# A retention layer and a gated MLP on one core: block 2 of the first MLP product goes from plain products to seven, under a new fixed order of all engines

## The chip, the cores and the metric

One core of a Trainium2 chip runs the whole program in one launch. The metric is the device time in microseconds (us), first to last instruction with what the launch adds around it. Five engines work side by side, each through its own list in order: TensorE (PE; its weight loads are PEld), VectorE (DVE), ScalarE (ACT), GpSimd (POOL) and SyncE (SP, which issues most DMAs). Waits between them go by semaphores.

## The reference

```python
scores = scale * np.matmul(q, k.transpose(0, 1, 3, 2))      # 8 batches, 8 heads, 576 x 64
Dmat = np.where(rel >= 0, gamma[:, None, None] ** rel[None, :, :], 0.0)
attn = np.matmul(scores * Dmat, v)                          # causal, decaying weights, no softmax
x = attn.transpose(0, 2, 1, 3).reshape(4608, 512)
h = x @ w_in                                                # 512 -> 2048
g = h * np.cos(h)
out = g @ w_out                                             # 2048 -> 512
```

All inputs and the output are float32.

## The kernel before

**Tiling.** The 4608 tokens are nine blocks of 512. A block is fed by two attention units of 256 tokens (`unit`, `scores`, `outputs`): q, k and v of a unit are loaded by SP (line 585), cast or weighted into `natk`, `qnat`, `natv` (lines 574, 575, 624), transposed (on PE at line 648 for the first four units, by DMA at line 663 for the rest), and multiplied in many small products of 64x64 tiles (line 694): scores (`bk<-qt,kt`), running states (`bk<-natv,natk`), outputs (`bk<-pt,natv`, `bk<-qt,sba` and its like). Two copies per unit write the block's `xt` (lines 574, 575).

**Layer 1** (x @ w_in, then g = h cos h) is made in one of two ways for each block j:

- Plain (`mlp1`, line 908): for each of 16 column groups f, four products over the contraction, 512 tokens wide. Blocks 0 (partly) and 1 are cut into token halves, products of 256. ACT takes the sine with a shift (line 917), DVE multiplies (line 920).
- In seven (`seven1`, line 1037): x and w_in are halved in both directions, and seven products of halves with sums of halves replace eight. A block is four groups g of seven steps of four products of 256, so 112 products. ACT copies three partial sums out of the banks per group (the `seed`, line 968, and two snaps, line 574), DVE adds two back (line 1020), the sines are line 1022, and the product h cos h is on DVE and POOL (line 1026). The sums of x (`xsums`, lines 961 and 963) are four DVE instructions per block.

The sums of w_in (`wsums1`, line 944) are made once: for each of two halves c, T1 and T7 on POOL, T2 and T4 on DVE. T7 is written in place over the slabs 2 and 3 of w_in, which the plain products read, so it waits for the last plain product; T1 carries a read of `xt` of the last plain block. `SEVEN` names the blocks in seven; before it is 3 to 8, and blocks 0, 1, 2 are plain.

**Layer 2** (g @ w_out) is in seven for all blocks (`wino2`, line 1177), with its own sums on DVE (lines 1086, 1108, 1114, 1166).

**Loads of the weights.** Four slabs of w_in and four of w_out (each 128x4x512, cast to bf16 on the way) are DMAs issued by POOL (`load_w`, lines 888 and 892). The loads of the units (0,1) and (1,1), which make block 1, wait for slab 2 of w_in and slabs 1 and 3; those of unit (2,0) wait for slab 2 of w_out.

**What sets the order.** `Graph` collects tasks; `lay` reads a rank for each task from the string `ORDER` (two characters a task), and each engine takes its tasks in rank order. `run` then plays the tasks through with a model of durations (among them `FETCH`, the model of when the next piece of PE's own code is there, `SHARES`, how the two kinds of DMA queues share, and the `dma=` and `tail=` of the slabs). What reaches the chip from that model: which buffer each task gets, how many filler products (`bk<-one`, 128x512, line 517) PE does where the model sees a gap, and which DVE instruction some POOL instructions wait for. The durations themselves reach nothing.

Of the kernel before, what the change touches and what calls it, by code (L numbers as in the profile page):

```python
# [11 lines left out]
B, H, S, D = 8, 8, 576, 64  # L12
# [87 lines left out]
def ap(t, size, p0, n, off, *dims):  # L100
    return bass.AP(t, p0 * size + off, [[size, n]] + [list(d) for d in dims])
# [29 lines left out]
class Graph:  # L131


    BACKLOG, FIRST = 4000, 6000
    SHARES = (0.65, 0.30)
    FETCH = (3200, 1500, 2550, 2000)
    SINCE = 3000

    def __init__(self, pools):
# [83 lines left out]
    def share(cls, hw, sw):  # L223
# [29 lines left out]
    def run(self):  # L253
# [3 lines left out]
        seen, usable, whole = 4, {}, [False] * 8  # L257
        dma_free, port_free = 2500.0, {"dve": 0.0, "pool": 0.0}
# [41 lines left out]
        while len(order) < len(self.tasks):  # L300
            s, e = min(((x, i) for i, x in ((e, due(e)) for e in free if todo[e]) if x is not None), key=lambda c: c[0], default=(0, None))
            if e is None:
                raise RuntimeError(f"the order is stuck: {[(e, todo[e][-1].name, [b.pool for b in todo[e][-1].allocs]) for e in free if todo[e]]}")
            t = todo[e].pop()
# [33 lines left out]
            if t.dma is not None:  # L338
                both = both and not (len(sw) == slow and ends[1][-1] < s)
                if not both:  # L340
                    dma_free = max(dma_free, s + 1750) + t.dma
                    done = dma_free + t.tail
                else:
# [11 lines left out]
                    if hw:  # L355
                        dma_free = ends[0][-1]
# [15 lines left out]
class Kernel:  # L372
# [43 lines left out]
    GATE = 'k'
    TXENG = ("pool", "dve", "pool", "dve")
# [480 lines left out]
    def mlp1(self, j, f, ses, prio):  # L898

# [25 lines left out]
    def wsums1(self):  # L925
# [12 lines left out]
        for c in range(2):  # L938
            for eng, i, x, y, r in (
# [4 lines left out]
                self.one(eng, 2150 if eng == "pool" else 660, lambda e, i=i, c=c, x=x, y=y: e.tensor_tensor(t(i, c), x(), y(), ALU.subtract),  # L944
                         r=r + self.xkeys(self.SEVEN[0] - 1, (0, 1)), w=keys(i, c), port=True, name=f"T{i}")

# [287 lines left out]
    def graph(self):  # L1234
# [116 lines left out]
```

## Time and profile before

| what | us |
|---|---|
| median of 3 runs | 282.84 (282.12 to 283.46) |
| the profiled execution, whole | 284.13 |
| its span, first to last instruction | 282.4 |
| PE matmul busy / PE weight load busy | 270.7 / 219.9 |
| DVE / ACT / POOL busy | 227.3 / 177.5 / 161.2 |
| HBM read and written | 36.70 MB, 9.44 MB |

The granted TensorE clock is 1.000 throughout. A row of the profile names the line, the engine, the tile written and the tiles read, the shape and the count; a time in brackets is idle time ahead of the group and what ended it. The chain of work that ended last goes back from the last instruction, at each step to what released it; its pieces in order of time show a start, a length and a name. "issue" means the engine waited for nothing that the profile shows. Matmul records overlap, so a rate is best read from the chain: the length of a run of products over their number.

### The profile page before, as it was taken

The numbers are of one execution on the slowest core, as the hardware profiler recorded it, in microseconds if no ns is written. First come the engines' busy times: TensorE is split into PE (matmuls) and PEld (weight loads), VectorE is DVE, ScalarE is ACT, GpSimd is POOL, SyncE is SP. The second block draws the span as 40 slices with busy tenths as digits, with TensorE's granted clock in tenths as the row PEclk, the third lists the DMA queues.
The fourth block names the chain that finished last, engine by engine and source line by source line (L and its number), as shares of the span: only waits on it lengthen the run. The fifth ranks groups of instructions, "written<-read, shape, count | busy, mean of one in ns | idle before, by whom it ended". The sixth has DMA issues, their size and how long they took to land.

```text
span 282.4 us, 9745 instructions
## 1 busy us (share of the span) xinstructions
PE 270.7 (96%) x4136; PEld 219.9 (78%) x4136; DVE 227.3 (80%) x394; ACT 177.5 (63%) x367; POOL 161.2 (57%) x180
## 2 busy tenths in 40 slices
PE   6779989999999999979999999999999999999995
PEld 2457568888885468868888888888888888888884
DVE  3666889988974998868997996688759899997764
ACT  4346767255247765669469875885778865778530
POOL 4640872167377683897568757981375667216330
DMA  7999999999999999999999997979816090410016
GB/s 199 249 192 262 273 171 163 300 243 263 179 187 245 204 264 206 181 221 176 251 192 208 279 238 134 168 194 175 194 32 123 6 163 2 159 69 0 2 74 224
DMA packets 122731, 49.91 MB, mean 177 GB/s; under 512 B 84800, under 2 KB 118592, under 8 KB 122688
## 3 DMA queue, kind: packets, MB, share of 16 engines
q1 hardware_dynamic: 118176, 44.84, 74.8%
q0 software_dynamic: 4224, 4.19, 9.6%
q8 instruction: 32, 0.52, 0.8%
q10 hardware_dynamic: 288, 0.26, 0.3%
q14 instruction: 11, 0.09, 0.1%
HBM read 36.70 MB, written 9.44 MB: 163 GB/s over the span
## 4 chain that ended last, share of the span: by engine, by line
PE 84%; DMA 8%; POOL 3%; issue 2%; SPq 1%; DVE 1%; ACT 1%; DVEq 0%; ACTq 0%
PE bk L1177 38%; PE bk L1037 26%; PE bk L908 11%; PE bk L694 8%; DMA stgq<-in_q_dram 3%; DMA win<-in_moe_w_in_dram 3%; DMA stgk<-in_k_dram 3%; POOL natv L624 1%; SPq L585 1%; POOL qnat L624 1%; POOL gt L1026 1%; POOL win L888 0%; ACT xt L574 0%; DVE sq L1020 0%; PE bk L648 0%
## 5 line engine op out<-in xcount | busy, mean ns | idle before, releaser
L1026 POOL TENSOR_TENSOR gt<-sq,cb 128x512 bf16<-128x512 f32 x48 | 55.8, 1172 | 49.1 <-ACT cb L1022 27.0
L908 PE MATMUL bk<-xt,win 128*128 128x256 bf16 (+1 forms) x288 | 46.3, 308 | 1.8 <-DMA win<-in_moe_w_in_dram 0.9
L624 POOL TENSOR_TENSOR natv<-stgv,wv 128x512 bf16<-128x512 f32 x36 | 37.5, 1046 | 12.5 <-DVE s L1108 4.8
L920 DVE TENSOR_TENSOR gt<-bk,cb 128x256 bf16<-128x256 f32 (+1 forms) x72 | 34.5, 507 | 12.0 <-ACT cb L917 9.3
L917 ACT ACTIVATE cb<-bk 128x256 bf16<-128x256 f32 (+1 forms) x72 | 31.2, 455 | 19.6 <-PE bk L908 16.5
L624 POOL TENSOR_TENSOR qnat<-stgq,wq 128x512 bf16<-128x512 f32 x32 | 33.5, 1052 | 16.7 <-DVE s L1114 5.6
L1037 PE MATMUL bk<-xt,win 128*128 128x256 bf16 x288 | 41.0, 273 | 0.0
L1020 DVE TENSOR_TENSOR sq<-bk,sq 128x512 f32<-128x512 f32 x48 | 32.5, 684 | 8.9 <-PE bk L1037 5.0
L908 PEld LDWEIGHTS bk<-xt,win 128*128 128x128 bf16 x288 | 26.8, 98 | 15.3 <-DVE pt L743 1.2
L743 DVE TENSOR_TENSOR pt<-bk,tr 128x512 bf16<-128x512 f32 x48 | 31.1, 682 | 8.4 <-PE bk L694 8.1
L575 POOL CAST natk<-stgk 128x512 bf16<-128x512 f32 x34 | 20.7, 614 | 28.2 <-DMA stgk<-in_k_dram 15.7
L1177 PE MATMUL bk<-wout,gt 128*128 128x256 bf16 x288 | 36.7, 273 | 0.0
L1026 DVE TENSOR_TENSOR gt<-bk,cb 128x512 bf16<-128x512 f32 x48 | 32.3, 682 | 4.0 <-ACT cb L1022 3.8
L1177 PE MATMUL bk<-wout,s 128*128 128x256 bf16 x288 | 35.6, 273 | 0.0
L1177 PE MATMUL bk<-tw,s 128*128 128x256 bf16 x288 | 35.4, 273 | 0.0
L574 ACT ACTIVATE sq<-bk 128x512 f32<-128x512 f32 x48 | 27.7, 595 | 10.0 <-PE bk L1037 8.8
L1022 ACT ACTIVATE cb<-sq 128x512 bf16<-128x512 f32 x48 | 30.0, 632 | 5.4 <-DVE sq L1020 2.9
L1022 ACT ACTIVATE cb<-bk 128x512 bf16<-128x512 f32 x48 | 28.4, 598 | 6.7 <-PE bk L1037 3.7
L1177 PEld LDWEIGHTS bk<-tw,s 128*128 128x128 bf16 x288 | 28.0, 98 | 3.6 <-DVE pt L743 0.3
L1037 PEld LDWEIGHTS bk<-xt,win 128*128 128x128 bf16 x288 | 27.9, 98 | 3.6
L1177 PEld LDWEIGHTS bk<-wout,gt 128*128 128x128 bf16 x288 | 27.6, 98 | 3.7 <-issue 0.2
L1177 PEld LDWEIGHTS bk<-wout,s 128*128 128x128 bf16 x288 | 27.7, 98 | 3.5
(80 smaller groups left out, 436.5 us busy)
## 6 DMA issues: line engine op xcount, KB each, us to landing
stgq<-in_q_dram SPq DMA_DIRECT2D x16, 512.0 KB, 6.1
out_dram<-os SPq DMA_DIRECT2D x16, 512.0 KB, 4.4
stgk<-in_k_dram SPq DMA_DIRECT2D x20, 256.0 KB, 5.6
stgv<-in_v_dram SPq DMA_DIRECT2D x20, 256.0 KB, 5.4
stgk<-in_k_dram SPq DMA_DIRECT2D x6, 512.0 KB, 6.9
stgv<-in_v_dram SPq DMA_DIRECT2D x6, 512.0 KB, 7.4
win<-in_moe_w_in_dram POOLq DMA_DIRECT2D x4, 512.0 KB, 8.0
wout<-in_moe_w_out_dram POOLq DMA_DIRECT2D x4, 512.0 KB, 7.5
```

The costliest lines, as they stand in the source:

```text
L574: return self.one(eng, dur, lambda e: e.activation(dst(), src(), AF.Copy), r=r, w=w, **kw)
L624: self.one(eng, 610 if eng == "dve" else 1030, lambda e, out=out, inp=inp, tab=tab, col=col, hs=hs: e.tensor_tensor(out(), inp(), ap(tab, ...
L694: return lambda e: e.matmul(out(), lhs(), rhs(), start=start, stop=True, skip_group_check=True)
L743: self.one("dve", 610, lambda e, r=r, b=b, pt=pt: e.tensor_tensor(ap(self.at(pt), 1024, 0, 128, 512 * r, [64 * ny * ny, 8 // ny // ny], [1 ...
L908: inst = e.matmul(ap(self.at(bk), 512, 0, 128, 0, [1, n]), ap(self.WIN, 4 * DFF, 0, 128, c * DFF + 128 * f, [1, 128]), ap(self.at(xt), 204 ...
L917: self.one("act", n - 15, lambda e: e.activation(ap(self.at(cb), TB, 0, 128, 0, [1, n]), ap(self.at(bk), 512, 0, 128, 0, [1, n]), AF.Sin, ...
L920: self.one("dve", 75 + n / 0.96, lambda e: e.tensor_tensor(ap(self.at(gt), NF * TB, 0, 128, f * TB + 256 * h0, [1, n]), ap(self.at(bk), 51 ...
L1020: self.one("dve", 610, lambda e: e.tensor_tensor(half(src), self.at(bank).ap(), half(src), ALU.add), r=[(bank,)], w=four(src))
L1022: self.one("act", 530 if name else 490, lambda e: e.activation(self.at(cb).ap(), ap(self.at(src), size, 0, 128, 0, [1, 512]), AF.Sin, bias ...
L1026: self.one(eng, 1120 if name else 610, lambda e: e.tensor_tensor(ap(self.at(gt), NF * TB, 0, 128, (8 * n + 2 * g) * TB + 256 * h, [TB, 2], ...
L1037: inst = e.matmul(ap(self.at(bank), 512, 0, 128, 256 * f, [1, 256]), l(c, f), rr(c), stop=True, skip_group_check=True, start=(first and f ...
L1177: inst = e.matmul(place(bank, tt), l(f, tt), rr(f), stop=True, skip_group_check=True, start=(first and f == 0 and tt < len(bank)))
```

## The change

`SEVEN` gains block 2. So its 64 plain products of 512 go, and 112 products of 256 come, with the copies, adds and sums of `seven1` and `xsums`; `wsums1` now has to be done a block earlier, after block 1 in place of block 2. `ORDER` is a new table for every engine and every task. `FETCH`, `SHARES` and the slab durations are new numbers of the model. Lines of the changed file are one higher than those of before (`seven1` is 1038 in place of 1037).

```diff
-    BACKLOG, FIRST = 4000, 6000
-    SHARES = (0.65, 0.30)
-    FETCH = (3200, 1500, 2550, 2000)
+    BACKLOG = 4000
+    SHARES = (0.80, 0.35)
+    FETCH = (3200, 1500, 3550, 5550)
...
-                    usable[k] = max(a + self.FETCH[0], dma_free + self.FETCH[1]) + self.FETCH[2] + self.FETCH[3] * (a < 45000)
+                    usable[k] = max(a + self.FETCH[0], dma_free + self.FETCH[1]) + self.FETCH[2 + (a < 45000)]
...
-    SEVEN = (3, 4, 5, 6, 7, 8)
+    SEVEN = (2, 3, 4, 5, 6, 7, 8)
...
-        "#####$#$#$#%#%#$#######%#&#&#%#$#&#'#)#(#'#)#,#+#'#.#7#/#*#/#'#+#*#,#(#-#.#&#&#%#*#)#(#-#(#)#*#0#2#0#1#3"
+        "#####$###$#$#&#$#####&#%#%#%#&#$#'#'#(#-#)#*#+#-#)#/#0#0#*#/#%#'#(#)#'#*#,#'#&#&#+#(#,#.#(#,#*#.#1#0#2#1"
...
-                 sem=f"{which}{s}", dma=2750 if which == "win" else 3000, tail=900, prio=prio)
+                 sem=f"{which}{s}", dma=3350 if which == "win" else 3450, tail=500, prio=prio)
```

The order on PE where block 1 begins. In before, after the outputs of unit (0,1), PE does a few plain products of block 0, one transpose of `qnat`, and then the plain products of block 1's first token half:

```order
L908 MATMUL bk<-xt,win 128x256 x4
L648 MATMUL bk<-idn,qnat 128x128 x4
L908 MATMUL bk<-xt,win 128x256 x28
L648 MATMUL bk<-idn,natk 128x128 x4
L908 MATMUL bk<-xt,win 128x256 x4
L1177 MATMUL bk<-wout,gt 128x256 x8
```

In the changed kernel block 0 is finished ahead of those outputs, and three transposes of unit (1,1) stand between them and block 1:

```order
L649 MATMUL bk<-idn,qnat 128x128 x4
L649 MATMUL bk<-idn,natk 128x128 x8
L909 MATMUL bk<-xt,win 128x256 x12
L695 MATMUL bk<-natv,natk 64x64 x16
L909 MATMUL bk<-xt,win 128x256 x20
L649 MATMUL bk<-idn,qnat 128x128 x4
```

So the transposes of `natk` moved ahead of block 1, into the place right after the outputs.

POOL around the sums of w_in (`tx<-win` is T1, `win<-win` is T7). In before they are spread among the casts of the units of blocks 3 to 5, and the last of the four stands a little further on:

```order
L624 TENSOR_TENSOR qnat<-stgq,wq 128x512
L944 TENSOR_TENSOR tx<-win 128x1024
L624 TENSOR_TENSOR qnat<-stgq,wq 128x512
L575 CAST natk<-stgk 128x512
L624 TENSOR_TENSOR qnat<-stgq,wq 128x512
L624 TENSOR_TENSOR natv<-stgv,wv 128x512
L575 CAST natk<-stgk 128x512
L624 TENSOR_TENSOR qnat<-stgq,wq 128x512
L624 TENSOR_TENSOR natv<-stgv,wv 128x512
L944 TENSOR_TENSOR win<-win 128x1024
```

In the changed kernel all four stand close together:

```order
L945 TENSOR_TENSOR tx<-win 128x1024
L576 CAST natk<-stgk 128x512 x2
L625 TENSOR_TENSOR qnat<-stgq,wq 128x512 x2
L576 CAST natk<-stgk 128x512
L945 TENSOR_TENSOR win<-win 128x1024
L625 TENSOR_TENSOR qnat<-stgq,wq 128x512 x2
L945 TENSOR_TENSOR tx<-win 128x1024
L625 TENSOR_TENSOR natv<-stgv,wv 128x512
L945 TENSOR_TENSOR win<-win 128x1024
```

So they moved some twelve POOL instructions forward, and eight POOL instructions of the seven products (line 1027) come behind them.

PE in the stage of block 2, where attention crowds most. In before (the scores and states of a unit between runs of products):

```order
L1177 MATMUL bk<-wout,s 128x256 x16
L1037 MATMUL bk<-xt,win 128x256 x4
L1037 MATMUL bk<-xs,tx 128x256 x4
L694 MATMUL bk<-qt,kt 64x64 x32
L694 MATMUL bk<-natv,natk 64x64 x16
L1037 MATMUL bk<-xt,tx 128x256 x4
L1037 MATMUL bk<-xs,tx 128x256 x4
```

In the changed kernel, behind the 80 small products of one unit's outputs and ahead of the 80 of the next, whose first 32 are the last row:

```order
L1038 MATMUL bk<-xt,win 128x256 x4
L1038 MATMUL bk<-xs,tx 128x256 x4
L1178 MATMUL bk<-wout,gt 128x256 x16
L695 MATMUL bk<-qt,kt 64x64 x32
L695 MATMUL bk<-natv,natk 64x64 x16
L1038 MATMUL bk<-xt,tx 128x256 x4
L1038 MATMUL bk<-xs,win 128x256 x4
L695 MATMUL bk<-pt,natv 64x64 x32
```

So between two runs of 80 small products there are now 48 small and 32 large ones, and between a unit's scores and its own outputs eight large ones.

More of the change, by code (lines that the diff above doesn't have):

```diff
@@ new lines @@
+        "#3#5#-#7#9#8#1#7#%#(#+#)#.#-#H#A#I#H#*#/#0#K#C#M#I#+#2#1#)#O#Q#K#L#N#O#P#G#T#S#U#J#S#,#7#6#X#N#W#K#-#;#4"
+        "#b#U#V#P#.#8#9#2#.#8#G#B#G#4#+#4#D#?#D#6#/#6#E#>#E#3#,#5#;#4#=#:#3#:#A#;#?#S#I#Q#>#7#@#9#2#9#=#6#;#<#5#<"
+        "#B#<#A#F#@#F#J#D#J#R#H#R#N#F#M#@#:#B#L#E#P#C#=#C#?#8#>#3#5#:#<#/#=#>#2#D#C#0#@#?#7#j#s#m#o#r#s#\\#\\#w#n#x"
+        "#a#b#]#b#i#k#`#j#w#n#Y#L#T$,#p$($.#r$+$-#q$*#u#`#v#|#e#|#p#^#p$+#s$,#e#X#c$/#t$-#q#_#u$$#g#z#Z#M#Y$0#u$."
+        "#[#O#W$1#v$0#f#Y#e$##i$##]#Q#X$4#w$1#a#T#^$2#x$2#`#W#_$'#k$$#y#c#y$%#h#{#_#V#d$*#o$'#z#d#x$)#m$)#^#R#Z$("
@@ new lines @@
+        "#l$%#V#[#U#\\#g#a#f#h#c#d#Z#k#m#l#i#n#]#g#h#[#r#t#t#l#o#q#Q#{$&#j#>#3#F#H#5#K#J#1#A#B#;$3$6$8$/$3$:#v#f$>"
+        "#{$#$?#|$$#6#8#I#L#:#O#N#9#4#Q#E#@#?#<#S#W#C#U#V#=#G#T#Z#H$=$A$>$=$?$@$F$)$,$G$($*$N$K$M$/$0$W$7$9$d$E$H"
+        "$e$F$Y#B#A#]#`#E#d#^#D#F#[#h#P#K#I#a#i#M#j#l#J#S#b#m#W$j$]$^$J$K$m$U$V$n$N$a#G$&#M$O#P$B#R$P$F$G$I$J$C$&"
+        "$K$+$E$'$E$M$.$R$N$6#Y$O$L$4#X$[$;$T$P$1$Q$2$X$8$S$S$3$V$Q$B#_$T$R$=#\\$]$>$W$U$5$\\$<$Y$@$X$Z$:$^$U$I#c$_"
+        "$V$P#f$a$C$_$`$?$g$G$c$D$Z$b$A$f$\\$M#e$l$`$R#g$k$L$b$4$6$5$7$;$C$<$A$7$8#y$5$9$9$;$<#z$:$@$%$B$D$D$H$J$H"
@@ new lines @@
+        "#N$I$L$-#v$c$e$g$h$o$O$r$S$q$T$m$s$W$w$o$_#n$u$j$[#r%$$Z$u%&$]%'$b%*$g$y%)$a%-$x$m#w%.$w$f#s%2$i$z%/$e%1"
+        "$h%3$k${%4$l%8%$$u#z%5%#$q#y%>$x%.%7$n%9$o%:$p%)%=$t%A%+${$#%<%'$y#|%E$z%2$[$f$d$i$k$t$l$s$h$i$Q$t$z$n$v"
+        "$x$X$p$y$Y${$|$p%0%6$|#\\%%%($`#Z%#$r$q$\\$^%+$j$d%,$c$v#O#L#k#q#R#u#t#U#_#o$$#]#V#T#p#x#Y#{$&#X#`#v$%#i%;"
+        "%%%&$s$r%?%%%,%@$v%(%*%,%0%/%C$w%I%#%H%$%6%G$|%K%3%1$,%L%5%+$*%N%'%=%Q%)%R%*%U%.%>%T%-%Z%C%5$.%Y%B%;$1%b"
+        "%8%F%\\%4%`%7%c%:%H%a%9%h%J%F$7%d%G%B$6%l%D%O%f%=%m%E%i%?%K%j%@%n%N%M$8%s%U%S$:%r%H%T%-%1%4%8%:%9%;%<%B%D"
@@ new lines @@
+        "%&%F%J%7%O%S%/%M%P%(%[%_%E%V%W%?#y%e%g%>#o%X%@%A%0%2%]%<%3%^%6%D#[#b$($2#^$+$'#e#d$0$)#l#a#c$/$-#h$9$5#f"
+        "#g$3$4#t%k%M%L%A%C%p%I%L%q%G%P%Q%S%W%V%t%J%v%P%w%N%X%x%O%{%]%V$?%|%\\%h$H&(%[%g&'%U&/%Z&+%Y%d&*%X&-%f%\\$A"
+        "&2%h%b$E&3%^%j&4%_&6%c&7%g%q&8%d&;%p%q$J&<%o%p$K&@%m%z&>%i&B%l&A%k%s&E%o&I%y%v$L&F%x%z$M&M%w&#%I%R%[%_%e"
+        "%`%b%a%o%u%K&)&,%c%y&.%]&#&&%W&5&9%l&0&1%i$.&=&?%j$4%z%Z%Y%Q%R&$%`%a&%%T%^#j#s$>$=#k$@$<#n#u$;$B#{#m#q$C"
+        "$G#r$I$D#p$*$F$N$(&:%m%n%e%f&C%s%{&D%n%t%u%w%{%v&G%r&L%u&K%y&&&N%x&Q&'&&$P&R&(%|$X&W&)&/&Y&'&Z&(&^&,&1&\\"
@@ new lines @@
+        "&*&`&2&.$S&]&0&/$U&f&3&6&d&0&h&4&j&6&<&g&5&l&:&;$[&k&9&=$]&r&@&D&m&8&p&<&x&F&H&q&:&w&B&C$^&u&A&I$_&|&D&F"
+        "%k%|&$&%%r&.&,&-&H&J%t&S&U&)&P&T&%&O&X&+&[&_&4&c&e&5$6&s&t&?$:&V&*&+&#&$&a&-&1&b&2&3$+#z#w#x$R$W#|$)$2$0"
+        "$V$Y$,$/$$$'$Q$O$;&i&7&8&7&n&o&9&;&=&>&C&?&v&>&y&A&z&B&E&{&E''&L&M$a'#&J&O$c'0&P&P'$&H'%&G')&J&K'*&K'.&M"
+        "&N$e'+&S&W$f'2&S&R',&L'6&V'/&U&U'1&Q'5&V&b$i';&Y&]$g'<&d&g'>&Y'?&Z'A&[&^'B&\\'E&f&f$j'C&`&^$h'O&h&m&@&I&G"
+        "&N&Q&Z&O&]'('3&T'4'7&T'8'9&X'&'-&R'='@&\\'H'J&h$?'D'F&_$A$%$-$#$&$T$Z$9$5$3$8$\\$`$1$=$7$<$d$b$>':&_&X&[&W"
@@ L415 @@
+        "'G&`&b&a&c&d&e&j&l'I&c'N&g'M&j&p'L&e'S&o&q$l'Q&n&l$k'V&p&x'R&i'T&k'Y&n&t'X&m']&v&t$m'W&s&x$n'b&v&{'Z&r'\\"
+        "&s'a'$'+'_&u'e'#'#$o'`&z'-$r'k'('-'c&w'i&z'h&|'''g&{'m'(''$p'l')'*$q'p'&',&a&k&r&w&i&q'$&y'P'U&o'K'[&u'^"
+        "'f&y'd'o'%'j'n'*'r't'/$@'s'w',$C&|'&'0'1'%'2'.'5'q'v')'+'u'|'3$F$B'y'z'/'.'x'{'0(#($'4'6$D$E(%(''8'1'2(&"
+        "(('7'9$G$H"
     )
```

28 lines of the change are left out of this document (removed).

## The prediction

> **What bounds the kernel now.** I read the page's busy times and slices first.
>
> ```profile
> span 282.4 us, 9745 instructions
> PE 270.7 (96%) x4136; PEld 219.9 (78%) x4136; DVE 227.3 (80%) x394; ACT 177.5 (63%) x367; POOL 161.2 (57%) x180
> PE   6779989999999999979999999999999999999995
> ```
>
> PE is below 9 tenths only in the first slices, once in the middle, and at the very end. The windows say how much is idle where (PE, PEld, DVE, ACT, POOL busy, then clock, DMA share, GB/s).
>
> ```profile
> 30.00:40.00 10.00, 8.85 (x161) 5.47 (x160) 8.31 (x17) 5.80 (x12) 9.77 (x12) 1.00 1.01 218
> ...
> 60.00:70.00 10.00, 10.00 (x93) 8.78 (x92) 9.27 (x21) 5.25 (x16) 5.75 (x7) 1.00 1.08 256
> 70.00:80.00 10.00, 9.97 (x218) 8.16 (x217) 9.79 (x17) 4.30 (x10) 4.32 (x6) 1.00 1.11 180
> ...
> 120.00:130.00 10.00, 8.54 (x247) 7.23 (x240) 7.01 (x12) 7.78 (x17) 8.54 (x10) 1.00 1.16 188
> ```
>
> The last idle of the start ends by 40 us, and after that the one hole over half a us is that of 120 to 130. Busy time alone would not prove it, since ends of matmuls are modelled; so I take the chain of waits in order of time.
>
> ```profile
> 12.95 8.27 DMA win<-in_moe_w_in_dram
> ...
> 21.70 8.43 DMA stgq<-in_q_dram
> 30.13 0.08 issue
> 30.21 1.76 POOL qnat L624 x2
> 31.97 0.26 issue
> 32.23 2.05 POOL natv L624 x2
> ...
> 37.51 0.71 issue
> ...
> 38.69 0.76 ACT xt L574
> 39.45 0.12 issue
> 39.57 3.22 PE bk L908 x28
> ...
> 69.50 0.44 PE bk L908 x4
> ...
> 85.55 3.45 PE bk L908 x16
> ...
> 123.99 1.46 issue
> ...
> 175.67 3.06 PE bk L1037 x28
> ```
>
> Up to 39.57 the chain runs through DMAs (a slab of w_in, then q of unit (0,1)) and POOL; from there it is PE almost without a break. The end is therefore the time at which block 1's first product starts, plus PE's work behind it, plus its few stalls.
>
> **The change, part by part.** All sums are against the profiled execution, 284.13 us whole, 1.29 above the median of 282.84; I carry the difference over to the median.
>
> *PE's work.* A 512-wide product costs 3.45/16 = 0.2156 us, a 256-wide one 3.06/28 = 0.1093 us. Removed: 64 x 0.2156 = 13.80. Added: 112 x 0.1093 = 12.24. So **-1.56 us**, all of it behind 39.57. The seeds of bank contents that the seven products need are ACT copies, not PE work. (The Trainium skill, "TensorE: Matmul & The Clock Gate", section "Back-to-back issue gap", speaks against the change: it gives a sustained stream about 131 ns for a product of 512 and 81 ns for one of 128, so width comes cheap. With some 98 ns between them for 256, an estimate from that page, the sum would be 112 x 98 - 64 x 131 = +2.6 us. This trace disagrees with it: 216 ns and 109 ns.)
>
> *The start.* The same eight slab and unit loads precede the first product of block 1. On POOL the second slab is now issued behind one cast (0.61) and one `natv` half (1.05, both by the page's groups below), the first slab ahead of a cast. PE gets there with more done: block 0 is finished and the transposes of `natk` are behind it, in what was idle of 30 to 40, where the window shows 1.15 us; two more 512-wide fillers and two more changes between small and large products lie in that idle too. I take **0** for the time of 39.57, with -0.6 (one cast earlier) to +1.66 (cast and `natv` in full) as bounds.
>
> *Work beside PE.* Durations by form:
>
> ```profile
> L1022 ACT ACTIVATE cb<-sq 128x512 bf16<-128x512 f32 x48 | 30.0, 632 | 5.4 <-DVE sq L1020 2.9 <-POOL gt L1026 1.8 <-DVE gt L1026 0.5
> ...
> L574 ACT ACTIVATE sq<-bk 128x512 f32<-128x512 f32 x48 | 27.7, 595 | 10.0 <-PE bk L1037 8.8 <-POOL gt L1026 1.2
> L1026 POOL TENSOR_TENSOR gt<-sq,cb 128x512 bf16<-128x512 f32 x48 | 55.8, 1172 | 49.1 <-ACT cb L1022 27.0 <-DVE xs L961 8.2 <-DVE s L1114 7.8
> L624 POOL TENSOR_TENSOR natv<-stgv,wv 128x512 bf16<-128x512 f32 x36 | 37.5, 1046 | 12.5 <-DVE s L1108 4.8 <-DVE s L1114 3.8 <-DMA stgv<-in_v_dram 2.5
> L575 POOL CAST natk<-stgk 128x512 bf16<-128x512 f32 x34 | 20.7, 614 | 28.2 <-DMA stgk<-in_k_dram 15.7 <-DVE pt L743 7.0 <-DVE s L1114 2.4
> ...
> L944 POOL TENSOR_TENSOR tx<-win 128x1024 bf16<-128x1024 bf16 x2 | 4.3, 2127 | 0.0
> ```
>
> ACT: the number of sines stays at 16, and 12 copies come: 12 x 0.595 = +7.1 us. POOL: 8 x 1.172 = +9.4 us. DVE: 16 products before, 8 products and 8 adds after, the same, and the four sums of x, about +2. ACT and POOL are at 63% and 57%, DVE at 80%; PE waits for none of them as long as each result is there in time, so **0**.
>
> *The sums of w_in, a block earlier.* T7 can't start before the last plain product of block 1, which in before ends at 69.50 + 0.44 = 69.94. By the order rows POOL then has T7, two `qnat`, T1, one `natv`, T7: 3 x 2.13 + 3 x 1.05 = 9.5 us, to about 79.5. By PE's order 112 products of 256 and 200 small ones of attention stand between the last plain product and the first that reads these sums.
>
> ```profile
> 77.28 1.30 PE bk L694 x76
> ```
>
> That is 112 x 0.1093 + 200 x 1.30/76 = 12.2 + 3.4 = 15.6 us, so the sums are needed near 85.6. Margin 6 us; POOL's queue behind T7 (casts for units of later blocks) has the idle of 60 to 80, where it is 5.75 and 4.32 busy of 10. So **0**; if the cover went, each us beyond the six would cost one.
>
> *Code.* PE's own instructions come in by DMA while it runs.
>
> ```profile
> q8 instruction: 32, 0.52, 0.8%
> ```
>
> That is 32 packets for 2 x 4136 instructions, 258 each, or 129 products. A piece that is late shows as "issue". The hole of 120 to 130 is such a one. One such packet passes in the 1.3 us of 122.6 to 123.9 (first row below, the queue's share of that stretch), and PE goes on behind it:
>
> ```profile
> q8 instruction: 1, 0.02, 5.5%
> ```
>
> ```profile
> 125.45 0.25 PE L694 MATMUL bk<-natv,natk 64*64 64x64 bf16 x7 [1.46 <-issue]
> ```
>
> The two of the start, 0.71 at 37.51 and another near 20, look alike. Density decides together with luck: 247 products in 120 to 130 stalled, 218 in 70 to 80 did not. In the changed order, the outputs of two units and the scores of one crowd: 80 + 8 + 16 + 48 + 8 + 80 products, 240, in
>
> ```profile
> 104.31 0.91 PE bk L694 x80
> ...
> 113.63 0.51 PE bk L694 x48
> ```
>
> 2 x 0.91 + 0.51 + 32 x 0.109 = 5.8 us. That is nearly two pieces of code in 5.8 us, where before had its densest ones at about 20 products per us (x218 in 10, x247 with a stall). So I expect a stall there, near 100 us, in place of the one at 124. Bounds: 0 (no piece late) to 2 x 1.46 = 2.9 (two late in a row). I take 1.5 times the one row, 2.2, since two pieces are in question and one stall gives the next piece time: **+0.7** against the 1.46 of before.
>
> *A unit's outputs close behind its scores.* The eight large products between them take 0.87; DVE needs two masks, which in before began 0.22 after PE.
>
> ```profile
> 114.20 1.29 DVE L743 TENSOR_TENSOR pt<-bk,tr 128x512 bf16<-128x512 f32 x2 [0.22 <-PE bk L694]
> ```
>
> 0.22 + 1.29 = 1.51, less 0.87 and about 0.2 for the states between: 0.4 us of wait, but inside the stretch where the code is late, so I count none of it beside that; bounds 0 and 0.4.
>
> The sum: -1.56 + 0 + 0.7 = **-0.9 us**, 283.2 profiled, **281.9** median.
>
> **The rivals.**
>
> *The code comes in time.* Then the 1.46 of before goes as well: -1.56 - 1.46 = -3.0, 279.8 (and any time between that and the forecast, if one piece is a little late). For it: of the stretches above, only one of before stalled past 40 us, and a planner that reckons with later code should leave more room. Against it: the 240 products in 5.8 us. (The Trainium skill, "Runtime: NRT & Kernel Launch", section "Instruction fetch mechanics", says the refill of 16 KiB blocks of 256 instructions is mostly hidden, and by it there would be no stall. The trace agrees on the size, 0.52 MB in 32 packets, and disagrees on the rest, by 1.46 us.) It shows as no "issue" over 0.5 us after 40. Everything faster than 281.4 belongs here: **0.34**.
>
> *Code late more often.* The other side: the same mechanism at four pieces, the two in the crowded stretch and two in later ones (before has the like of the x205 here). 4 x 1.46 = 5.8; against 1.46 that is +4.4, with -1.56 it is +2.8: 285.6. It decides from two more late pieces on, since 2 x 1.46 is above 1.56. For it: the DMA share is above 1 in that row (1.27) as in most up to 170, so a packet has a queue ahead of it.
>
> ```profile
> 150.00:160.00 10.00, 9.80 (x205) 8.32 (x203) 8.75 (x13) 9.34 (x21) 7.99 (x9) 1.00 1.27 212
> ```
>
> Against it: one late piece shifts PE and gives the next more time. **0.17**.
>
> *POOL late with T7*, over its 6 us: the seven products of block 2 stand and everything with them; 10 us late gives +4 - 1.56 = +2.4, 285.2. The margin speaks against it: **0.02**.
>
> *Wide products cheaper than two narrow ones.* In a stream a product can't be below its weight load, 219.9/4136 = 0.053 on average; if the 64 wide ones in truth cost half of 0.2156 each, the change would lose 12.24 - 6.9 = +5.3. The 16 in 3.45 us exclude it nearly: **0.02**.
>
> *The start is late* by 1.66 us, which eats the gain of PE: 282.84 + 0.8 = 283.6, within 0.5% of before, **0.03**.
>
> **How the numbers follow.** Forecast 0.42, code in time 0.34, code late more often 0.17, POOL 0.02, wide products 0.02, late start 0.03. A measurement of this kernel can tell about 0.5%, 1.41 us, from no change. Faster than 281.4: 0.34. Slower than 284.25: 0.17 + 0.02 + 0.02 = 0.21. Within: 0.45. The forecast's own range goes from -1.56 - 0.6 (start) - 0.5 (a stall of about 1 in place of 1.46) = -2.7 to -1.56 + 1.44 (two late pieces) + 0.4 (masks) + 0.4 (a quarter of the start's bound) = +0.7, so 280.2 to 283.5; to hold 8 in 10 it takes in most of the faster rival, down to 280.0, and half of the slower, up to 284.8.
>
> **What would show it.** Right: in the chain, products of line 1038 at 0.109 us in the stage of block 2; the first product of block 1 within 0.6 of 39.57; PE without idle behind it but for "issue" near 100; the hole of DVE in 80 to 90, in which the plain block of before left it 4.61 busy of 10, filled.
>
> ```profile
> 80.00:90.00 10.00, 10.00 (x171) 6.92 (x170) 4.61 (x8) 4.89 (x11) 8.22 (x8) 1.00 1.18 222
> ```
>
> Wrong: PE waiting for POOL `win` or DVE `tx` near 86 (the sums late), for DVE `pt` by over 0.4, or a slab of w_in that lands after 22.5.

## The result, and the profile after

The changed kernel took 286.67 us in the median of 4 runs (284.91 to 286.94), the kernel before 283.15 in 4 runs beside it (282.12 to 283.50): a ratio of 1.0107, 95% interval 1.0068 to 1.0146. It is slower, by about 3.0 us. The prediction said 281.9, with a range of 280.0 to 284.8. The profiled execution took 286.94, its span is 285.2.

The head of the page of the changed kernel:

```profile
span 285.2 us, 9866 instructions
PE 273.6 (96%) x4186; PEld 224.0 (79%) x4186; DVE 231.3 (81%) x398; ACT 183.2 (64%) x379; POOL 171.7 (60%) x188
PE   7879999999999999999999999999999999999995
PE 75%; DVE 10%; DMA 5%; ACT 3%; POOL 2%; issue 2%; SPq 1%; DVEq 0%; POOLq 0%
```

PE is still busy 96% of the time, and the slices look full. What has changed is the last line, the shares of the chain that ended last. In before it read

```profile
PE 84%; DMA 8%; POOL 3%; issue 2%; SPq 1%; DVE 1%; ACT 1%; DVEq 0%; ACTq 0%
```

So 10% of the chain now goes through DVE and 3% through ACT, where it was 1% each. A share of the chain is not lost time: part of it lies near 130 to 144 and 187 to 199 us, where PE loses only 0.45 and 0.26. Windows of the changed kernel, most of them those of the prediction (PE, PEld, DVE, ACT, POOL busy, clock, DMA share, GB/s):

```profile
60.00:70.00 10.00, 9.74 (x103) 8.24 (x100) 6.80 (x18) 8.06 (x22) 8.74 (x9) 1.00 1.02 202
70.00:80.00 10.00, 9.71 (x188) 7.76 (x176) 9.95 (x16) 2.65 (x7) 5.34 (x6) 1.00 1.09 231
80.00:90.00 10.00, 9.84 (x199) 8.15 (x197) 9.19 (x15) 6.52 (x15) 6.76 (x5) 1.00 0.99 184
90.00:100.00 10.00, 9.52 (x141) 7.41 (x141) 8.95 (x14) 9.01 (x20) 9.12 (x10) 1.00 1.01 213
100.00:110.00 10.00, 9.02 (x244) 6.96 (x232) 9.02 (x15) 8.61 (x18) 7.45 (x8) 1.00 0.91 196
120.00:130.00 10.00, 9.98 (x185) 8.06 (x185) 6.43 (x11) 8.82 (x19) 9.26 (x10) 1.00 1.15 176
```

The hole of 120 to 130 is gone. In its place there are short ones from 60 to 110 us, and from 90 to 110, where block 2 is now made in seven, DVE and ACT are near nine tenths, and POOL is up to 100 us. What PE waits for behind 45 us, from the waits of the changed kernel (idle us in all, times, longest):

```profile
PE bk L695 <- issue: 0.7, 1, 0.7
PE bk L1178 <- DVE s L1109: 0.5, 2, 0.3
PE bk L695 <- DVE pt L744: 0.4, 1, 0.4
PE bk L1038 <- issue: 0.3, 1, 0.3
PE bk L909 <- DVE gt L921: 0.3, 1, 0.3
PE bk L1038 <- ACT sq L575: 0.2, 1, 0.2
PE bk L1038 <- ACT bk L969: 0.2, 1, 0.2
PE bk L1038 <- DVE sq L1021: 0.2, 1, 0.2
PE bk L695 <- ACT xt L575: 0.2, 1, 0.2
```

In before there was one row:

```profile
PE bk L694 <- issue: 1.7, 2, 1.5
```

These lists are short of the truth, since the modelled ends of matmuls cover part of each wait (the 0.69 of code near 162 is 0.87 by the starts). So I add up from the starts of all products: what lies between one start and the next, less the length of a product (0.1092 for 256, 0.0108 and 0.0165 for the small ones, and so on) and less 0.1 at each change between small and large ones, is **lost time**. The sums below are worked out from these starts; a small negative one only means that the mean length is a little high. Two profiles of each kernel (the second ones are experiments 9 and 5 below):

| us | before | before, again | changed | changed, again |
|---|---|---|---|---|
| first product of block 1 | 39.57 | 39.30 | 40.34 | 39.31 |
| lengths of all products from there | 232.26 | 232.26 | 230.18 | 230.18 |
| changes between small and large (60 and 64) | 6.0 | 6.0 | 6.4 | 6.4 |
| lost up to 45 | 0.12 | 0.12 | 0.22 | 0.22 |
| lost 45 to 80 | 0.32 | 0.35 | 1.04 | 1.82 |
| lost 80 to 110 | -0.15 | -0.33 | 2.35 | 2.00 |
| lost 110 to 170 | 1.31 | 0.67 | 1.24 | 1.45 |
| lost behind 170 | -0.03 | -0.07 | 0.01 | -0.10 |
| start of the last product | 279.28 | 278.20 | 281.68 | 281.18 |
| span | 282.4 | 281.3 | 285.2 | 284.7 |

Means of the two: start +0.4, lengths -2.1, changes +0.4, lost time +4.0 (1.16 to 5.13), last product to end +0.4; together +3.1, as the spans have it (281.85 to 284.95). The gain on PE came as forecast, and was eaten nearly twice over by lost time, most of it between 45 and 110 us. Not all of that is waiting for DVE and ACT: of the 2.35 from 80 to 110 us, 0.48 is a piece of PE's code that came late at 109.13 ("issue"), and 0.49 is the masks (DVE `pt` at 105.28). About 1.4 is left for copies, seeds, adds and sums.

The chain of the changed kernel names the places:

```profile
72.71 2.44 DVE s L1109 x3
...
93.52 2.74 PE bk L1038 x24
...
96.27 0.61 ACT sq L575
...
98.01 0.59 ACT bk L969
...
103.94 1.29 DVE pt L744 x2
...
161.68 0.69 issue
...
216.87 4.80 PE bk L1038 x44
```

From 40 us on before's chain was PE and a little issue, but for 259 to 264 us, where it ran through DVE, POOL and ACT. Here it leaves PE for a sum of layer 2 on DVE (72.71), a copy out of a bank (96.27), a seed (98.01), the masks (103.94). The last row is the rate of seven products where nothing disturbs them: 4.80/44 = 0.109 us.

### The profile page after: what moved, and what is told of

It is laid out like the page before. It is cut to its first block, busy times and chain, and to the rows that moved or that the text cites. A ratio compares the mean times of both kernels' runs of the same rounds, so it can differ in the third digit from the quotient of the medians.

```text
span 285.2 us, 9866 instructions
## 1 busy us (share of the span) xinstructions
PE 273.6 (96%) x4186; PEld 224.0 (79%) x4186; DVE 231.3 (81%) x398; ACT 183.2 (64%) x379; POOL 171.7 (60%) x188
## 4 chain that ended last, share of the span: by engine, by line
PE 75%; DVE 10%; DMA 5%; ACT 3%; POOL 2%; issue 2%; SPq 1%; DVEq 0%; POOLq 0%
PE bk L1178 33%; PE bk L1038 26%; PE bk L909 9%; PE bk L695 7%; DMA win<-in_moe_w_in_dram 3%; DMA stgv<-in_v_dram 2%; DVE s L1109 2%; DVE pt L744 2%; POOL gt L1027 1%; DVE xs L962 1%; DVE sq L1021 1%; ACT cb L1023 1%; ACT sq L575 1%; SPq L586 1%; ACT xt L575 1%
## 5 line engine op out<-in xcount | busy, mean ns | idle before, releaser
L1027 POOL TENSOR_TENSOR gt<-sq,cb 128x512 bf16<-128x512 f32 x56 | 65.2, 1169 | 47.4 <-ACT cb L1023 23.6
L1038 PE MATMUL bk<-xt,win 128*128 128x256 bf16 x336 | 48.9, 273 | 0.2 <-DVE sq L1021 0.2
L1027 DVE TENSOR_TENSOR gt<-bk,cb 128x512 bf16<-128x512 f32 x56 | 38.1, 683 | 8.1 <-ACT cb L1023 6.0
L575 ACT ACTIVATE sq<-bk 128x512 f32<-128x512 f32 x56 | 33.1, 602 | 9.3 <-PE bk L1038 8.1
L1023 ACT ACTIVATE cb<-sq 128x512 bf16<-128x512 f32 x56 | 35.2, 634 | 5.6 <-DVE sq L1021 4.4
L1038 PEld LDWEIGHTS bk<-xt,win 128*128 128x128 bf16 x336 | 31.6, 98 | 5.3 <-DVE sq L1021 0.3
L1038 PE MATMUL bk<-xs,tx 128*128 128x256 bf16 x224 | 33.2, 273 | 0.6 <-issue 0.3
L909 PE MATMUL bk<-xt,win 128*128 128x256 bf16 (+1 forms) x224 | 31.1, 288 | 2.4 <-DVE gt L921 1.1
L575 ACT ACTIVATE sn<-bk 128x512 f32<-128x512 f32 (+1 forms) x29 | 16.4, 568 | 25.0 <-PE bk L1178 21.2
L918 ACT ACTIVATE cb<-bk 128x256 bf16<-128x256 f32 (+1 forms) x56 | 22.3, 416 | 14.5 <-PE bk L909 11.3
```

The lines of the kernel that those rows point to most:

```text
L575: return self.one(eng, dur, lambda e: e.activation(dst(), src(), AF.Copy), r=r, w=w, **kw)
L909: inst = e.matmul(ap(self.at(bk), 512, 0, 128, 0, [1, n]), ap(self.WIN, 4 * DFF, 0, 128, c * DFF + 128 * f, [1, 128]), ap(self.at(xt), 204 ...
L918: self.one("act", n - 15, lambda e: e.activation(ap(self.at(cb), TB, 0, 128, 0, [1, n]), ap(self.at(bk), 512, 0, 128, 0, [1, n]), AF.Sin, ...
L1023: self.one("act", 530 if name else 490, lambda e: e.activation(self.at(cb).ap(), ap(self.at(src), size, 0, 128, 0, [1, 512]), AF.Sin, bias ...
L1027: self.one(eng, 1120 if name else 610, lambda e: e.tensor_tensor(ap(self.at(gt), NF * TB, 0, 128, (8 * n + 2 * g) * TB + 256 * h, [TB, 2], ...
L1038: inst = e.matmul(ap(self.at(bank), 512, 0, 128, 256 * f, [1, 256]), l(c, f), rr(c), stop=True, skip_group_check=True, start=(first and f ...
```

## The experiments

**Theory A**: the changed kernel loses its gain, and more, in short waits of PE for DVE and ACT, because the seven products' copies, adds and products come into a stage where both engines have no room; one further cause is a POOL instruction that holds up a bf16 sum on DVE. **Rival B**: late code. **Rival C**: 112 products of 256 cost PE more than their count says. A further rival came up on the way: the new order, and not block 2 in seven, makes the waits. Ratios are to the kernel before, run beside it on the same chip, with the 95% interval; "lost" is the sum above, of the one execution that was profiled. Where a kernel leaves out work, the expectation says so.

**1. T7 ahead of the cast.** POOL's order:

```diff
 L625 TENSOR_TENSOR qnat<-stgq,wq 128x512 x2
-L576 CAST natk<-stgk 128x512
 L945 TENSOR_TENSOR win<-win 128x1024
+L576 CAST natk<-stgk 128x512
```

> The changed kernel with one place changed in POOL's order: the first T7 stands ahead of the cast of natk that waits for its DMA, not behind it. Theory A (PE of the changed kernel loses its gain in short waits for DVE and ACT, at 66 to 82 us and at 93 to 107 us; one cause is a POOL instruction that holds up a bf16 sum on DVE): the first sum of layer 2 of block 1 falls from 1.85 us to about 0.7, and the excess of 0.32 and 0.33 us ahead of PE's products at 75.7 and 78.1 goes: 0.6 us less in the profile at 80 us, ratio to before about 1.008 in place of 1.0107. Rival B (late code makes the loss): the two waits stay or come back as others, no gain. Rival C (the 112 products themselves are slower than the 64): no gain.

Between 71 and 76 us the first two sums of layer 2 of block 1 and T7 stand like this in the changed kernel (busy, mean ns of one):

```profile
L1109 DVE TENSOR_TENSOR s<-gt 128x1024 bf16<-128x1024 bf16 x2 | 2.4, 1262 | 0.0
L945 POOL TENSOR_TENSOR win<-win 128x1024 bf16<-128x1024 bf16 x1 | 2.1, 2121 | 0.0
...
L576 POOL CAST natk<-stgk 128x512 bf16<-128x512 f32 x1 | 0.6, 611 | 1.0 <-DMA stgk<-in_k_dram 1.0
```

and in this kernel

```profile
L1109 DVE TENSOR_TENSOR s<-gt 128x1024 bf16<-128x1024 bf16 x2 | 1.3, 684 | 0.0
```

Lost from 45 to 80: 0.17 in place of 1.04; from 80 to 110 it is 2.32, as before the edit. Ratio 1.0091 (1.0058 to 1.0124), within the interval of the changed kernel. So T7, put off by 1.0 us by a load of k, did stretch the sum by 2 x (1.262 - 0.684) = 1.2 us, and the two waits behind it went. But experiments 2 and 4 have the old place and lose 0.30 and 0.17 there: with a load that lands earlier the collision doesn't happen; the cast does not stand there, and the pair of sums takes 1.28 us in both. It is a cost of some executions, not the cause of the 3 us.

**2. Adds of block 2 cut.**

```diff
-self.one("dve", 610, lambda e: e.tensor_tensor(half(src), self.at(bank).ap(), half(src), ALU.add),
+m = 32 if j == 2 else 512
+self.one("dve", 610, lambda e: e.tensor_tensor(  # columns 0 to m of the same three
```

> The changed kernel with the eight adds of block 2's seven products on DVE cut to 32 of 512 columns (most of those two sums per group is left out): about 8 x 0.6 = 4.8 us less work on DVE between 88 and 108 us. Theory A, DVE being what is late there: the excess at 105.3 (0.59, the masks) and 106.5 (0.40, an add) goes, and part of that at 98.6: 0.8 to 1.2 us less. Theory A, ACT being what is late: less than 0.3. Rival B: the waits for code at 109.1 and 162.4 (0.48 and 0.87) stay and nothing else matters: within 0.3. Rival C: no gain.

Ratio 1.0084 (1.0055 to 1.0114); lost from 80 to 110: 2.02 against 2.35. The masks' wait stays (0.49), the seed's too. Some 4.8 us less for DVE (14.55 busy of 20 from 90 to 110 in place of 17.97) is not enough; the expectation that DVE alone is late is wrong.

**3. Sines and snaps of block 2 cut.**

```diff
+m = 64 if j == 2 and g > 1 else 512     # snaps: columns copied
+w = 64 if j == 2 and g > 0 else 512     # sines: columns
```

> The changed kernel with block 2's sines of groups 1 to 3 and snaps of groups 2 and 3 cut to 64 of 512 columns (most of g h cos h of these is left out): 12 x 0.5 + 4 x 0.5 = 8 us less work on ACT between 91 and 108 us. Theory A with ACT late: the excess at 96.9 (0.41, a snap) and 98.6 (0.40, a seed) goes, 0.8 us less. Theory A with DVE late: these shrink little, under 0.3. Rival B and rival C: no gain.

Ratio 1.0066 (1.0037 to 1.0094), lost from 80 to 110: 2.14. The wait for a snap at 96.9 went, the others stayed, and the late code at 109 is 0.69 here. ACT's sines alone aren't it either: ACT is 12.35 busy of 20 from 90 to 110, as little as in before (12.51), and most of the loss is still there.

**4. Code shifted by 32 products.**

```diff
+extra = 0 if self.shifted else 32
+self.shifted = True
 def mm(e):
+    for _ in range(extra):
+        e.matmul(...)   # bk<-one, 128x64
     for _ in range(n):
```

> The changed kernel with 32 tiny products more at the very start, where PE idles, so that every later piece of PE's code begins 32 products earlier in the program. Rival B: the late piece at 162.4 gets 7.0 us of PE work between its request and its use in place of 5.5, so its 0.87 us go, and the one at 109.1 (5.4 us, as before) stays: 0.8 us less, ratio about 1.008. Theory A: as rival B for these 0.87 us, and all other waits stay; over 2 us of the loss remain. If the time falls by more than 1.5 us, theory A is wrong.

Ratio 1.0137 (1.0101 to 1.0174): not faster. The two waits for code, 0.32 at 109.13 and 0.69 at 162.37 in the changed kernel, are two larger ones here:

```profile
106.04 0.22 PE L701 MATMUL bk<-qt,sbb 64*64 64x64 bf16 x2 [1.32 <-issue]
```

```profile
173.77 0.49 PE L1184 MATMUL bk<-wout,gt 128*128 128x256 bf16 x3 [0.90 <-issue]
```

The late piece at 162 did go, as rival B has it, but others came, so the shift moved the late code and did not remove it. The masks' wait (0.49), the snap's and the seed's stayed, as A has it. The time of this run can't be read as the price of code alone: in its profile the granted clock was 0.5 for 3.4 us from 107.7 on (0.77 in the window from 105 to 110), and eight products of 256 that take 0.87 at full clock took about 1.7 there. That is some 1.7 of the 4.93 us lost from 80 to 110, and three of the five executions behind the ratio have a mean clock of 0.992 to 0.994.

**5. The changed kernel again** (no edit).

> The changed kernel itself, once more. Theory A (short waits of PE for ACT and DVE, fixed by the order): the waits at 94 to 98 us (about 1.0 us in all), behind the scores at 104 to 106 (about 0.8) and the two for code (about 109 and 161) recur in the new profile. Those at 68 to 80 us (1.2 in the first profile) recur only if the order alone makes them; if they hang on when a DMA lands, they do not. Ratio 1.007 to 1.011. Rival: the loss is chance of one profile, then the waits stand elsewhere and the ratio is under 1.005.

Ratio 1.0125 (1.0090 to 1.0159). The loss is not chance. What recurs: the seed (98.06), the masks at 104.7, the add behind them, and late code near 162. The snap's wait does not (0.14 at 96.3), and near 109 nothing is put down to code:

```profile
PE bk L695 <- issue: 1.1, 1, 1.1
PE bk L1178 <- DVE tw L1087: 0.7, 1, 0.7
PE bk L695 <- DVE pt L744: 0.6, 2, 0.4
PE bk L909 <- DVE gt L921: 0.5, 1, 0.5
PE bk L1038 <- ACT bk L969: 0.2, 1, 0.2
PE bk L1038 <- DVE sq L1021: 0.2, 1, 0.2
```

From 45 to 80 it loses 1.82, in another way than the first profile: sums of w_out at 48.8 (row two) and `gt` behind T2 at 68 (row four), not T7. In the nine profiles of kernels with this order, 45 to 80 lost from 0.16 to 1.82; 80 to 110 always over 1.1, and the masks' wait was 0.47 to 0.49 in eight of the nine.

**6. Block 2 in seven under another order**, one laid out with later loads and later code assumed, so that more room is left behind them.

```diff
-        "#####$###$#$#&#$#####&#%#%#%#&#$#'#'#(#-#)#*#+#-#)#/#0#0#*#/#%#'#(#)#'#*#,#'#&#&#+#(#,#.#(#,#*#.#1#0#2#1"
+    ORDER = (...)   # all 30 lines new; nothing else
```

> Block 2 in seven as in the changed kernel, the same tasks, but another order on all engines, laid out with loads and code assumed later. Theory A (the places in the order make the waits): waits of PE behind 45 us fall from 4.9 to under 3.5 us, ratio to before 1.000 to 1.005. Rival C (seven products cost PE more than their count says, whatever the order): ratio stays at 1.008 or more.

Ratio 1.0101 (1.0074 to 1.0127), lost 4.29 in all. The waits moved (1.6 at 89.4, for a `natv` whose load was late, and 0.7 for masks at 105.7) but did not go. The expectation of A on the order was wrong. The 3.21 lost from 80 to 110 is made up otherwise than in the changed kernel, though: half of it is that one load.

**7. All side work of block 2 cut** (the edits of 2 and 3, and):

```diff
-self.seed(A, Bb)
+self.seed(A, Bb, j == 2)      # 32 of 512 columns
+v = 16 if j == 2 else 256     # columns per half of each product h cos h
```

> The changed kernel with everything that DVE, ACT and POOL do for block 2's seven products cut short (seeds, adds and products to 32 columns, sines and snaps from the second and third group on to 64; most of h and g of block 2 is left out). Theory A: the waits at 94 to 99 us (about 1.0 us) go, since ACT's copies and DVE's adds are what banks wait for; the wait behind the scores (0.49 at 105, for the masks) and those for code stay or grow: 1 us less, ratio about 1.006. Rival B (code alone): nothing goes but by chance, and the sum of the waits is within 0.3 of the changed kernel's.

Ratio 1.0024 (0.9992 to 1.0057), against 1.0125 (1.0090 to 1.0159) for the changed kernel run beside it: about 1.0%; the medians are 284.21 and 286.59, 2.4 us apart. PE's list of products is the same. Behind 45 us it waits for

```profile
PE bk L695 <- DVE pt L744: 0.6, 2, 0.4
PE bk L1187 <- DVE xt L576: 0.3, 1, 0.3
PE bk L1047 <- issue: 0.3, 1, 0.3
PE bk L695 <- issue: 0.3, 1, 0.3
```

and no more for snaps, seeds or adds. This decides against C (the products are as many and as long) and against B alone. The gain is larger than expected: lost from 80 to 110 is 1.18, but from 45 to 80 it is only 0.16, which block 2 has no part in, and waits for code are shorter too. So about 0.8 to 1.2 us of the gain is the stage itself (1.18 against 2.35 and 2.00), and the rest is not laid to one cause. The waits that stay there are for the masks (0.49), for a copy to `xt` (0.46) and for code at 106.5 (0.46).

**8. Block 2 plain under a new order**, laid out as in 6, with all of the changed kernel's model numbers (of these, `FETCH` is shown).

```diff
-    FETCH = (3200, 1500, 2550, 2000)
+    FETCH = (3200, 1500, 3550, 5550)
-    ORDER = (...)
+    ORDER = (...)   # all 29 lines new; block 2 stays plain
```

> The kernel before (block 2 plain), with its order laid out anew in the same way and with the changed kernel's model numbers. Theory A: what the order costs or gives is separate from block 2's form, so this one gains as well, ratio 0.990 to 0.998, mostly because the late piece of code at 125 us (1.64) is gone. Rival: the order of before has nothing to give, ratio 1.000.

Ratio 1.0006 (0.9982 to 1.0030): no gain, where A expected one. In its profile the late piece of code came at 83 us (idle 1.5) and others at 126.9 and 163.0 (0.7 each); but that execution, 285.52, is the slowest of its twelve, and it doesn't tell what the median holds. Apart from that code it loses nothing from 80 to 110. With 6 this makes a square: under orders laid out in the same way, block 2 in seven is 1.0101 and plain 1.0006, nearly as far apart as the changed kernel and before. So it is the seven products, and not this one order, as far as two orders can show it.

**9. The kernel before, again** (no edit).

> The kernel before, profiled once more, to see what in its account is chance. Theory A: behind 45 us PE waits only for code (in the first profile 1.64 us at 125, 0.2 to 0.3 at 152, 171, 212 and 264), so the sum of its waits is again under 2.5 us; where the late piece of code is, and whether there is a second, may differ. Rival (the waits of the changed kernel are chance): waits for ACT and DVE of 0.3 us and more stand in this profile too.

One execution, 283.06 us; lost 0.74 in all. Its waits behind 40 us:

```profile
PE bk L694 <- issue: 0.9, 1, 0.9
PE bk L1177 <- DVE pt L743: 0.2, 1, 0.2
```

The piece at 125 was late again, by less. No wait for ACT or DVE reaches 0.3, so the waits of the changed kernel are not chance of the profile.

**10. ACT's part of block 2 cut** (3, and the seeds of 7), and **11. DVE's and POOL's part cut** (2, and the products of 7). The edits in words:

```diff
+seed: 32 columns for j == 2; snaps and sines: 64            # 10
+adds: 32 columns for j == 2; products h cos h: 16 per half  # 11
```

> The changed kernel with ACT's part of block 2's seven products cut short (seeds to 32 of 512 columns, sines and snaps to 64 from the second and third group on; most of h and g of block 2 is left out), DVE and POOL as they were. If ACT is what makes the loss that went with everything short (ratio 1.0024 against 1.0125 for the changed kernel): ratio 1.002 to 1.005, and the waits at 94 to 99 gone. If DVE and POOL make it: ratio 1.009 or more. If both do: 1.005 to 1.009.

> The changed kernel with DVE's and POOL's part of block 2's seven products cut to 32 of 512 columns (adds and the products h cos h; most of g of block 2 is left out), ACT as it was. If DVE and POOL make the loss: ratio 1.002 to 1.005, and the masks at 104 us start no later than before but the wait of 0.30 behind them goes. If ACT makes it: 1.009 or more, with the waits of 0.4 at 97 and 98 us still there. If both do: 1.005 to 1.009.

1.0070 (1.0042 to 1.0098) and 1.0074 (1.0049 to 1.0099): by these both count, and neither alone gives what both together give (1.0024), though the intervals touch. Lost from 80 to 110: 2.03, and 3.23 of which 1.65 is code late at 108.9, against 1.18 with everything cut. The stage of 90 to 110 us: before, the changed kernel, everything cut, ACT cut, DVE and POOL cut, in this order.

```profile
90.00:110.00 20.00, 20.00 (x336) 12.67 (x335) 19.24 (x32) 12.51 (x27) 12.65 (x12) 1.00 1.16 218
```

```profile
90.00:110.00 20.00, 18.53 (x361) 14.37 (x359) 17.97 (x29) 17.63 (x37) 16.56 (x17) 1.00 0.96 204
```

```profile
90.00:110.00 20.00, 18.97 (x369) 15.61 (x368) 10.62 (x29) 11.55 (x37) 8.75 (x17) 1.00 1.00 213
```

```profile
90.00:110.00 20.00, 18.54 (x361) 14.60 (x360) 17.93 (x29) 11.81 (x38) 14.61 (x17) 1.00 1.03 198
```

```profile
90.00:110.00 20.00, 17.33 (x350) 13.57 (x349) 11.13 (x28) 16.53 (x35) 11.58 (x19) 1.00 1.02 197
```

Before had a full DVE there (19.24 of 20) and an ACT with room (12.51); that was enough for PE to run through. In the changed kernel both are near 18. With ACT cut DVE is still there, and PE's waits from 100 to 110 are for DVE (adds, the sums of x of block 3):

```profile
PE bk L1044 <- DVE xs L962: 0.7, 2, 0.4
PE bk L1044 <- DVE sq L1025: 0.6, 2, 0.3
```

With DVE cut ACT is at 16.53, the seed is waited for, and this profile has a piece of code late by 1.5 us besides.

Busy time in the stage does not settle it. With ACT cut, ACT (11.81) and DVE (17.93) are both below what before had (12.51 and 19.24), and PE still loses 2.03; experiment 3 says the same (12.35, 17.90, lost 2.14). So two full helpers are not a condition of the loss. What the waits name is single results that the products need and that come late.

**12. More ACT work in the kernel before.**

```diff
-self.one("act", n - 15, lambda e: e.activation(...), r=[(bk,)], w=[(cb,)])
+sine = (n - 15, lambda e: e.activation(...), [(bk,)], [(cb,)], {})
+self.G.add("act", n - 15, [sine] * (2 if j == 2 and f % 4 > 0 else 1))
```

> The kernel before, block 2 plain, with the sine of twelve of block 2's sixteen groups done twice: 12 x 0.6 = 7.2 us more on ACT in the stage of block 2, as much as the twelve copies of the seven products, and each result 0.6 us later, with PE's products and order untouched. If more ACT work in that stage is enough to make PE wait: waits of PE behind banks appear at 90 to 105 us, ratio 1.003 to 1.008. If it takes the seven products' own chain (copy, then a product into the same bank): no wait over 0.2 there, ratio 1.000.

Ratio 1.0082 (1.0052 to 1.0112), 2.3 us, with PE's products and order untouched. Lost from 80 to 110: 2.02, against -0.15 and -0.33 in the two profiles of before.

```profile
PE bk L694 <- issue: 0.8, 1, 0.8
PE bk L908 <- DVE gt L921: 0.7, 3, 0.3
PE bk L694 <- ACT sbb L574: 0.5, 1, 0.5
PE bk L1178 <- DVE gt L921: 0.2, 1, 0.2
```

```profile
90.00:110.00 20.00, 19.03 (x324) 10.76 (x318) 17.22 (x29) 18.04 (x38) 12.64 (x12) 1.00 1.00 242
```

So 7.2 us more on ACT, with results 0.6 later, brings about as much lost time into this stage as the change did, none of it code or masks, and brings ACT to the same 18 of 20. Whether the fullness or the delay does it this kernel doesn't separate; that the seven products' own chain isn't needed for it, it shows.

## Why the prediction was wrong, step by step

- **PE's work, -1.56**: right. Each product kept its 0.109 us, and the lengths from block 1's first product on fell by 2.08: the 1.56, and 0.5 that had moved into the head. Wide products cheaper than two narrow ones: no.
- **The start, 0 with -0.6 to +1.66**: +0.77 in one profile, 0.0 in the other. Inside the bounds.
- **Changes between small and large products**, put into the idle of the head: 0.4 of them were behind it. A small miss.
- **Work beside PE, 0: this step failed.** The prediction gave the added work (7.1 us on ACT, 9.4 on POOL, 2 on DVE), held it against shares of the whole span, 63, 57 and 80%, and took each result to be there in time. It was not: from 80 to 110 PE lost 2.0 to 2.35 us in place of none. In the first profile 0.49 of the 2.35 are the masks and 0.48 late code (steps below), so about 1.4 belongs to this term; in the second the masks are 0.49 of 2.00, and 0.44 near 108.5 has no named cause. Experiment 7 shows the cause: with this work cut and PE's products as they were, the ratio falls from 1.0125 to 1.0024 and the stage's loss by 0.8 to 1.2. Experiment 12 shows that added ACT work alone can do it. Held against the stage, the sum would at least have warned: 12.51 + 7.1 = 19.6 of the 20 us of ACT from 90 to 110, with DVE at 19.24. It would not have given the price, as experiments 3 and 10 show.
- **The sums of w_in a block earlier, 0**: PE never waited for them, so the rival that POOL is late for them did not come true. But the margin of 6 us was not there. The second T7 began at 84.60, behind a wait for DVE, and ended at 86.7, where the forecast had 79.5:

```profile
84.60 2.12 POOL L945 TENSOR_TENSOR win<-win 128x1024 bf16<-128x1024 bf16 x1 [1.83 <-DVE s L1115]
```

  The first of PE's products that need it (`bk<-xs,win`) began at 89.56, 2.8 us later, and the last sum on DVE ended at 93.88, 0.9 ahead of the first `bk<-xt,tx`. And a bill came elsewhere, which the step did not look at: T2 waits on DVE for T1, and block 1's `gt` are queued behind it, as the changed kernel's row on DVE shows:

```profile
66.47 1.07 DVE L945 TENSOR_TENSOR tx<-win,tx 128x1024 bf16<-128x1024 bf16 x1 [0.47 <-POOL tx L945]
```

  PE lost 0.42 there, and 0.71 in the second profile, and T7 stretched layer 2's sum (experiment 1). Together that is 0 to 1.1 us from one execution to the next. For T7 it was a load of k; what sets it for T2 is not shown.
- **Masks behind the scores, 0.4 but not counted**: 0.49, in eight of nine profiles, and beside the late code, not inside it. It should have been counted.
- **Code, +0.7**: code is late near 109 and 162 in one profile (idle 0.32 and 0.69) and near 162 in the other (1.1), against 1.7 and 0.9 in before: -0.7 to +0.2. The term was too large by 0.5 or more. The crowded stretch near 100 did not stall as forecast; the nearest wait is the 0.32 behind it. The rival "code late more often" gave a time near the truth (285.6), but not its mechanism.
- **The end**: 0.4 more from the last product to the end of the span, which was not foreseen and not tried out.

What stays open: how much of the 45 to 80 us loss belongs to the change. It is 1.04 and 1.82 in the two profiles of the changed kernel, 0.16 to 0.30 in four of the others with its order, and 0.60 to 1.79 in the other three. Open too is whether a helper's fullness or a single late result makes PE wait from 80 to 110.

## What to carry to other kernels

When work moves from one engine to others, look at those engines in the stage where it falls, not in the whole span. A sum that fills the stage is a warning and no price: here a DVE at 19.24 of 20 did no harm in before, and a DVE at 17.93 beside an ACT at 11.81 did in experiment 10. So ask for each result that the bounding engine waits on when it will be there. Saving 1.56 us of that engine is little if it puts some 18 us of work on the others. And an order that has a consumer close behind its producer (scores, masks, outputs) should be charged for that wait wherever the row for it stands in the trace.

## What was not expected of the hardware

A bf16 sum on DVE that began at 72.62 us, while POOL was in T7 (71.80 to 73.92), took 1.85 us and ended 0.55 behind T7; the pair took 2.4 us, and 1.3 in experiment 1, where T7 did not overlap it. The Trainium skill, "SBUF — State Buffer", section "SBUF: two separate sides", says that DVE with two operands in SBUF and GpSimd share a port pair which the first one holds for its whole instruction; the trace agrees, by the 1.262 against 0.684 us of experiment 1.

A change between products on 64x64 tiles and full ones costs PE about 0.1 us by the starts of products in both kernels, so 6.0 and 6.4 us for the 60 and 64 of them from block 1's first product on. The Trainium skill, "TensorEngine Tiling (Array Packing)", section "Key Properties", says a change of tiling mode drains the engine; the trace fits that, and gives the change a size.

PE's code arrives in pieces of some 258 instructions (32 packets for 2 x 4136). Where a piece is late recurs, and by how much varies: the piece at 125 us of before was late by 1.46 and 0.9 in two executions and by 0.8 in experiment 12, and eight of the nine profiles with the changed kernel's order lose 0.46 to 1.28 us near 159 to 162. The ninth is experiment 4, where 32 more products ahead of everything gave waits of 1.32 and 0.90 at other places.
